# A three-matrix stage without decode steps in a block's first product, and with one operand load issued later

## The chip, the cores and the metric

The kernel runs on one core of a Trainium2 chip. The time of a kernel is the device time of one execution in microseconds (us); of several runs the median counts. Times inside a profile are microseconds from the start of the profiled span.

## The reference, cut to what matters

An attention with decay comes first, then two feed-forward networks. The stage that is changed here computes the inner part of the second one, three products of the same x with three weight matrices and the largest of the three, element by element:

```
def _moe2_ref(x, w1, w2, w3, w_out) -> np.ndarray:
    h = np.maximum(np.maximum(x @ w1, x @ w2), x @ w3)
    return (h @ w_out).astype(np.float32)
```

x is 3072 x 512, each of w1, w2, w3 is 512 x 768, all float32. The weights reach the kernel as 64-bit numbers, two 32-bit words each, and the kernel decodes them into float32 itself.

## The kernel before, in words

**Products.** Each large matrix product is done by a seven-product scheme on 2 x 2 blocks (Strassen's form): seven products q0 to q6 of sums of blocks take the place of eight. To keep float32 precision on TensorE, an operand is split in a high part (ScalarE, a cast, L254) and the rest (VectorE, a subtraction, L255), and three matmuls take the place of one: high x high, high x low, low x high (L876 to L878).

**Order of the changed stage.** The outer loop is over three passes j (`GH = 3`): each pass has its own third of the columns of all three weight matrices. In a pass three blocks n go through (`NB = 3`), each a third of the tokens. In a block run the seven products q. A product has three parts p, one for each weight matrix, each of six matmuls into one bank of PSUM. The text numbers the 63 products of the stage 0 to 62 (`s = 7 * blk + q`, `blk = 3 * j + n`) and the parts 1 to 3. Everything is issued by hand in program order; each engine runs its own instructions in that order, and so does each DMA queue (SP's, and the one that ScalarE issues).

**Banks.** Six banks form two sets of three, "a" and "b", which swap roles from block to block. `ORDER` says which set a product writes and whether it starts it afresh: q0 a, q1 b, q2 a, q3 b, q4 a, q5 b, q6 a; q0 and q3 start afresh, and in block 0 q1 does. In all other blocks q1 accumulates onto what the copies of q0 (L881, ScalarE) have put into the set b: that set was the "a" of the block before, so a copy of q0 has to wait until the last product of the block before, q6, has been read out of that bank (L891 on ScalarE for part 1, maxima of L889 on VectorE for parts 2 and 3). q0 writes the set that was "b" before, so it waits for the evictions of q5 (L895, VectorE).

**Operands.** The split operands lie in HBM (`spill`) and are loaded again for every pass. In pass 0 operands 8 to 20 are still made in the stage (`make_op`: cast on ScalarE, subtraction on VectorE, store by SP). From operand 21 on they are loaded by `op_load`, 1 MB each, up to operand 24 on SP's queue, from operand 25 on on ScalarE's. When product s ends, the operand that next uses its buffer (`heir[s]`) is loaded: six products later in pass 1 (six buffers), four products later in pass 2 (four buffers).

**Decode steps.** While a pass runs, the weights of the next are decoded (in the last pass: the output weights). Six pieces of 512 KB are fetched into three buffers and go through `step`, which alternates `decode_a` and `decode_b`. A piece is taken up by `decode_front` (L124 on ScalarE, which waits for the piece to land, and L126 on GpSimd), goes through L147 and L149 on VectorE (`decode_a`), L156 on ScalarE (`decode_b`) and L141 on VectorE (the next `decode_a`). When a piece is finished, `due` rises by one, and the next `decode_b` issues a fetch for each one due, on ScalarE's queue (`due_more`, L93). In addition the first block of a pass issues a fetch at the head of q0, q2 and q4, on SP's queue, and sets the count of those due to zero:

```
if n == 0 and q in (0, 2, 4):
    due[0] = 0
    more()
```

`Spread(jobs, slots)` hands out the steps: `side.tick()` is called once a part, and at tick t as many jobs are done as len(jobs) * t / slots, rounded up. The first two jobs are idle, then come 12 steps; the last pass adds a `drain` and seven pieces (`wogen`) that split the output weights on ScalarE (L211) and VectorE (L212). In passes 0 and 1 the decoded weights are split at the ends of the products of the third block (`wgen`).

Of the kernel before, what the change touches and what calls it, by code (L numbers as in the profile page):

```python
# [33 lines left out]
GH = 3  # L34
# [13 lines left out]
def fused_kernel(ctx: ExitStack, tc: tile.TileContext, ck, w12, w3t, wo1, w123, wo2, mask, gout, gch, kdec, out):  # L48
# [16 lines left out]
    def spill(n, q):  # L65
        return opsp[n, q].rearrange("h p x -> p h x")

    def halves(t):
        return t.bitcast(F32).rearrange("p (h x) -> p h x", h=2)

    def stage_pool(name, side="left"):
        st = ExitStack()
        return st, pool(st, name, side=side, reuse_waits="tile")
# [15 lines left out]
    def fetch(src, raw, hi=None, lo=None, st=None):  # L89
        k = stage_turn[0]  # L90
        stage_turn[0] += 1
        st = ring[k % len(ring)] if st is None else st
        (nc.scalar if late[0] else nc.sync).dma_start(out=st.bitcast(I64), in_=src)  # L93
        loaded.append((st, dec_t[k % 2][:, :], raw, hi, lo))
# [138 lines left out]
    def raw_quads(n):  # L233
        return [wraw_t[0][:, i * n:(i + 1) * n] for i in range(4)]
# [177 lines left out]
    def fetch_w123(j, w, u):  # L412
        raw = wraw_t[0][:, :4 * GH * 256].rearrange("p (q i n) -> p q i n", q=4, i=GH)
        fetch(w123[j, w, u], raw[:, 2 * u:2 * u + 2, w, :])
# [8 lines left out]
    with tc.manual_schedule():  # L423
# [129 lines left out]
        side = Spread([idle] * 5 + [step] * (4 * GA), 4 * (12 + LAG))  # L553
        wgen = weights(raw_quads(1024), 1024)
        for g in range(KF // GA):
            for n in range(NB):
                blk = g * NB + n
                sets = sets_b(blk)
                for q in range(7):
                    s = 7 * blk + q  # L560
# [5 lines left out]
                    t = s + 3  # L566
# [49 lines left out]
                    if z == 6:  # L616
# [11 lines left out]
                        side = Spread([idle] * 3 + [step] * 36, 4 * (7 * NB - LAG))  # L628
# [45 lines left out]
        side = Spread([step] * 12, 8 * ZD)  # L674
# [42 lines left out]
        J1, J2 = 7 * NB, 14 * NB  # L717
        home_h = [z % 4 for z in range(J1)] + [(4, 5, 1, 2, 3, 0)[z % 6] for z in range(J1)] + [(2, 3, 0, 1)[z % 4] for z in range(J1)]
        bufs_h = [x[:, :] for x in op_t]
        heir = {s: next((t for t in range(s + 1, 7 * NB * GH) if home_h[t] == z), None) for s, z in enumerate(home_h)}  # L720

        def op_load(t):
            eng = nc.sync if t < J1 + 4 else nc.scalar
            eng.dma_start(out=halves(bufs_h[home_h[t]]), in_=spill(t // 7 % NB, t % 7))  # L724
# [3 lines left out]
        side = Spread([idle] * 4 + [step] * (4 * GH), 26)  # L728
        wgen = weights(raw_quads(256 * GH), 256 * GH)
        GEN = (15, 18, 21, 24, 27, 30, 33, 36)  # L730
        XL = 0
        for s in range(XS):
            n, r = divmod(s, 14)
            q, kk = divmod(r, 2)
# [90 lines left out]
        for j in range(GH):  # L825
            if j == GH - 1:
                xc_st.close()
                xb_st.close()
            if j + 1 < GH:
                wq += [lambda w=w, u=u: fetch_w123(j + 1, w, u) for w in range(GH) for u in range(2)]  # L830
                side = Spread([idle] * 2 + [step] * (4 * GH), 2 * 21 + 3)
            else:
                o_st, o_pl = stage_pool("o")
                wo = [o_pl.tile([P, 2, 768], F32R, name=f"wo{q}") for q in range(7)]
                raw = wraw_t[0][:, :].rearrange("p (m u k n) -> p m u k n", m=2, u=2, k=3)
                wq += [lambda k=k: fetch(wo2[k], raw[:, :, k // 3, k % 3, :]) for k in range(KH)]
                wogen = weights(raw_quads(768), 768, lambda q, n: wo[q])
                side = Spread([idle] * 2 + [step] * (2 * KH) + [drain]
                              + [lambda q=q: wogen(q) for q in (0, 1, 5, 2, 3, 4, 6)], 2 * 21 + 6)
            wgen = weights(raw_quads(256 * GH), 256 * GH)  # L840
            for n in range(NB):
                blk = j * NB + n
                sets = {"a": hbank[blk % 2], "b": hbank[1 - blk % 2]}
                m11, m21, m12, m22 = m_t[blk % 2]
                for q in range(7):
                    s = 7 * blk + q
                    if s < XL:
                        xwgen(7 - XL + s)
                    if s == 0:
                        op_load(3)  # L850
                    if PH[q] < 0:
                        make_op(s, quad_h, len(GEN))
                    if j == GH - 1 and n == NB - 1:
                        if q == 3:
                            o_load(0, 0, 0)
                            o_load(0, 0, 1)
                        elif q == 4:
                            o_load(0, 1, 0)
                            o_load(0, 1, 1)
                        elif q == 5:  # L860
                            o_split(0)
                        elif q == 6:
                            o_split(1)
                            o_pre(2)
# [3 lines that stand above are left out]
                    which, first = ORDER[q]  # L868
                    x = quads4(bufs_h[home_h[s]])
                    w = wslot(q, 256 * GH).rearrange("p h (i k n) -> p h i k n", i=GH, k=2)  # L870
                    seeded = blk > 0 and q == 1
                    for p in range(GH):
                        ps = sets[which][p]
                        for k in range(2):
                            wh, wl = w[:, 0, p, k, :], w[:, 1, p, k, :]
                            nc.tensor.matmul(ps, wh, x[:, 0, k, :], start=first and k == 0 and not seeded, stop=False, skip_group_check=True)  # L876
                            nc.tensor.matmul(ps, wh, x[:, 1, k, :], start=False, stop=False, skip_group_check=True)  # L877
                            nc.tensor.matmul(ps, wl, x[:, 0, k, :], start=False, stop=k == 1, skip_group_check=True)  # L878
                        u, c, e = (part(nm, p) for nm in "UCE")
                        if q == 0:  # L880
                            nc.scalar.copy(out=sets["b"][p] if blk else u, in_=ps)  # L881
                        elif q == 2:
                            nc.scalar.copy(out=c, in_=ps)
                        elif q == 3:
                            nc.scalar.copy(out=e, in_=ps)
                        elif seeded or q == 6:
                            m = m12 if q == 6 else m11
                            if p:
                                nc.vector.tensor_tensor(out=m, in0=m, in1=ps, op=ALU.max)  # L889
                            else:  # L890
                                nc.scalar.copy(out=m, in_=ps)  # L891
                        else:
                            m, v, (x0, x1), op = {1: (m11, u, (u, ps), ALU.add), 4: (m22, e, (ps, e), ALU.subtract),
                                                  5: (m21, c, (c, ps), ALU.subtract)}[q]
                            nc.vector.tensor_tensor(out=v if p else m, in0=x0, in1=x1, op=op)  # L895
                            if p:
                                nc.vector.tensor_tensor(out=m, in0=m, in1=v, op=ALU.max)
                        if p == GH - 1:
                            if s == 12:
                                xc_st.close()  # L900
                                xc_st, xc_pl = stage_pool("x2o")
                                bufs_h += [xc_pl.tile([P, 2048], F32R, name=f"opx{z}")[:, :] for z in range(2)]
                            if s in (12, 13):
                                op_load(J1 + s - 12)
                            t = heir[s]
                            if t is not None and not len(GEN) <= t < J1:
                                op_load(t)
                        if p == PH[q]:
                            make_op(s, quad_h, len(GEN))
                        side.tick()  # L910
                    if q == 1:
                        store(hsp[n, 0, :, j, :], m11)
                    elif q == 4:
                        store(hsp[n, 1, :, j + 3, :], m22)
                    elif q == 5:
                        store(hsp[n, 0, :, j + 3, :], m21)
                    elif q == 6:
                        store(hsp[n, 1, :, j, :], m12)
                    stores()
                    if n == NB - 1 and j + 1 < GH:  # L920
                        if q == 0:
                            side.rest()
                            drain()
                        wgen(q)
            side.rest()
# [6 lines left out]
        for s in range(7 * NB):  # L932
            n, q = divmod(s, 7)
# [99 lines left out]
```

## Time and profile before

| | |
|---|---|
| median of three runs | 820.87 us (819.47 to 821.22) |
| the profiled execution | 818.6 us |
| its span, first to last instruction | 816.6 us |
| TensorE matmul, weight load | 805.8 us (99%), 672.5 us (82%) |
| VectorE (DVE) | 631.9 us (77%) |
| ScalarE (ACT) | 389.1 us (48%) |
| GpSimd (POOL) | 76.0 us (9%) |
| the changed stage | about 468 to 726 us of the span |

In the profile PE is TensorE's matmul, PEld its weight load, which runs beside the matmuls; DVE, ACT, POOL and SP are the other engines, and ACTq and SPq stand for what these issue themselves, mostly DMAs. A row of a timeline has the start, the duration, the engine, the line of the kernel, the operation, the tile written and those read; in square brackets stands how long the engine was idle before it, and what it waited for.

### The profile page before, as it was taken

What the parts mean: (1) busy time and instruction counts of PE and PEld (TensorE: products, weight loads), DVE (VectorE), ACT (ScalarE), POOL (GpSimd) and SP (SyncE); (2) the same over time, 40 slices, a digit from 0 to 9 for tenths busy, and PEclk for the clock granted to TensorE, in tenths of its full rate; (3) what the DMA queues carried; (4) which work ended last, traced back from release to release, by engine and by line L of the source; (5) the groups of instructions that cost most, each with busy time, mean ns of one, the idle gap of its engine ahead of it and who ended that gap; (6) DMA issues with size and microseconds to landing.
All of it is one profiled execution on the core that took longest, in us unless ns stands there. A gap on an engine that the chain in (4) does not pass through costs nothing. (4 is left out here: it accounts for less than half of the span.)

```text
span 816.6 us, 12214 instructions
## 1 busy us (share of the span) xinstructions
PE 805.8 (99%) x4648; PEld 672.5 (82%) x4648; DVE 631.9 (77%) x795; ACT 389.1 (48%) x589; POOL 76.0 (9%) x93
## 2 busy tenths in 40 slices
PE   8999999999999999999999999999999999999997
PEld 8889888888888888888888888888888888888886
DVE  3799899989698978679799848993665555588782
ACT  2432646463345454567577545453334334444642
POOL 2443000000011111001010001000000010000000
PEclk9999999999999999999999999999999999999999
DMA  9998698799999975686789798989998699956522
GB/s 346 407 407 309 226 365 344 274 342 330 388 334 417 352 307 182 241 298 212 269 301 350 275 347 306 369 292 417 394 318 306 239 335 351 326 210 215 193 104 78
DMA packets 70154, 246.56 MB, mean 302 GB/s; under 512 B 6608, under 2 KB 6736, under 8 KB 70096
## 3 DMA queue, kind: packets, MB, share of 16 engines
q1 hardware_dynamic: 48864, 165.97, 53.8%
q10 hardware_dynamic: 21232, 79.81, 27.4%
q8 instruction: 37, 0.61, 0.3%
q14 instruction: 21, 0.17, 0.1%
HBM read 163.97 MB, written 81.79 MB: 301 GB/s over the span
## 5 line engine op out<-in xcount | busy, mean ns | idle before, releaser
L577 PE MATMUL bank<-op,w 128*128 128x512 f32 x336 | 130.8, 389 | 0.0
L579 PE MATMUL bank<-op,w 128*128 128x512 f32 x336 | 130.7, 389 | 0.0
L578 PE MATMUL bank<-op,w 128*128 128x512 f32 x336 | 130.7, 389 | 0.0
L876 PE MATMUL bank<-op,w 128*128 128x512 f32 x330 | 128.6, 390 | 0.1
L878 PE MATMUL bank<-op,w 128*128 128x512 f32 x330 | 128.4, 389 | 0.0
L877 PE MATMUL bank<-op,w 128*128 128x512 f32 x330 | 128.4, 389 | 0.0
L126 POOL TENSOR_SCALAR dec<-dec 128x512 f32<-128x512 f32 x64 | 48.5, 757 | 552.8 <-ACT dec L124 516.1
L577 PEld LDWEIGHTS bank<-op,w 128*128 128x128 f32 x336 | 63.1, 188 | 13.3 <-issue 0.2
L578 PEld LDWEIGHTS bank<-op,w 128*128 128x128 f32 x336 | 63.1, 188 | 13.2
L579 PEld LDWEIGHTS bank<-op,w 128*128 128x128 f32 x336 | 63.1, 188 | 12.9
L876 PEld LDWEIGHTS bank<-op,w 128*128 128x128 f32 x330 | 61.9, 188 | 13.9 <-ACT bank L881 0.9
L878 PEld LDWEIGHTS bank<-op,w 128*128 128x128 f32 x330 | 61.9, 188 | 12.8
L877 PEld LDWEIGHTS bank<-op,w 128*128 128x128 f32 x330 | 61.9, 188 | 12.8
L752 PE MATMUL bank<-op,w 128*128 128x512 f32 x168 | 65.4, 389 | 0.0
L750 PE MATMUL bank<-op,w 128*128 128x512 f32 x168 | 65.4, 389 | 0.0
L751 PE MATMUL bank<-op,w 128*128 128x512 f32 x168 | 65.4, 389 | 0.0
L156 ACT ACTIVATE dec<-stg 128x512 int32<-128x512 uint32 x49 | 33.1, 676 | 52.4 <-DVE stg L149 46.0
L147 DVE TENSOR_SCALAR dec<-dec 128x512 int32<-128x512 int32 x64 | 27.0, 421 | 21.8 <-POOL dec L126 21.8
L124 ACT ACTIVATE dec<-stg 128x512 f32<-128x512 f32 x49 | 32.6, 665 | 13.2 <-DMA stg<-in_w_dram 7.4
L889 DVE TENSOR_TENSOR m<-m,bank 128x512 f32<-128x512 f32 x34 | 23.3, 684 | 19.6 <-PE bank L878 19.0
L948 PE MATMUL bank<-w,wo 128*128 128x512 f32 x96 | 37.4, 390 | 0.0
L947 PE MATMUL bank<-w,wo 128*128 128x512 f32 x96 | 37.4, 389 | 0.0
(216 smaller groups left out, 1581.8 us busy)
## 6 DMA issues: line engine op xcount, KB each, us to landing
op<-opsp ACTq DMA_DIRECT2D x53, 1024.0 KB, 8.1
opsp<-op SPq DMA_DIRECT2D x34, 1024.0 KB, 5.6
ck<-in_ck_dram SPq DMA_DIRECT2D x34, 512.0 KB, 10.0
fsp<-C SPq DMA_DIRECT2D x24, 512.0 KB, 4.8
op<-opsp SPq DMA_DIRECT2D x10, 1024.0 KB, 6.0
hsp<-m SPq DMA_DIRECT2D x32, 256.0 KB, 6.3
stg<-in_w_dram SPq DMA_DIRECT2D x15, 512.0 KB, 9.4
U<-fsp SPq DMA_DIRECT2D x14, 512.0 KB, 5.9
```

What stands on the lines that cost most here:

```text
L126: nc.gpsimd.tensor_scalar(out=df, in0=df, scalar1=MAX_HI, scalar2=MIN_HI, op0=ALU.min, op1=ALU.max)
L577: nc.tensor.matmul(ps, wh, x[:, 0, k, :], start=first and k == 0 and not seeded, stop=False, skip_group_check=True)
L578: nc.tensor.matmul(ps, wh, x[:, 1, k, :], start=False, stop=False, skip_group_check=True)
L579: nc.tensor.matmul(ps, wl, x[:, 0, k, :], start=False, stop=k == 1, skip_group_check=True)
L750: nc.tensor.matmul(ps, wh, x[:, 0, k, :], start=first and kk == 0 and k == 0, stop=False, skip_group_check=True)
L751: nc.tensor.matmul(ps, wh, x[:, 1, k, :], start=False, stop=False, skip_group_check=True)
L752: nc.tensor.matmul(ps, wl, x[:, 0, k, :], start=False, stop=kk == 1 and k == 1, skip_group_check=True)
L876: nc.tensor.matmul(ps, wh, x[:, 0, k, :], start=first and k == 0 and not seeded, stop=False, skip_group_check=True)
L877: nc.tensor.matmul(ps, wh, x[:, 1, k, :], start=False, stop=False, skip_group_check=True)
L878: nc.tensor.matmul(ps, wl, x[:, 0, k, :], start=False, stop=k == 1, skip_group_check=True)
L947: nc.tensor.matmul(ps, wh[:, k, o], xh[:, k], start=first and k == 0, stop=False, skip_group_check=True)
L948: nc.tensor.matmul(ps, wh[:, k, o], xl[:, k], start=False, stop=False, skip_group_check=True)
```

## The change

In the last two passes, and in the first one from its second block on, no tick is made in q0. The number of slots is set to 39, 36 and 39 for the three passes, where it was 45, 45 and 48. The load that stood at the end of q6 (for the buffer that q6 has freed) is issued at the end of the next block's q0, ahead of q0's own load.

```
@@ -828,7 +828,7 @@
             if j + 1 < GH:
                 wq += [lambda w=w, u=u: fetch_w123(j + 1, w, u) for w in range(GH) for u in range(2)]
-                side = Spread([idle] * 2 + [step] * (4 * GH), 2 * 21 + 3)
+                side = Spread([idle] * 2 + [step] * (4 * GH), (39, 36)[j])
@@ -836,7 +836,7 @@
                 side = Spread([idle] * 2 + [step] * (2 * KH) + [drain]
-                              + [lambda q=q: wogen(q) for q in (0, 1, 5, 2, 3, 4, 6)], 2 * 21 + 6)
+                              + [lambda q=q: wogen(q) for q in (0, 1, 5, 2, 3, 4, 6)], 39)
@@ -902,12 +902,14 @@
                             if s in (12, 13):
                                 op_load(J1 + s - 12)
-                            t = heir[s]
-                            if t is not None and not len(GEN) <= t < J1:
-                                op_load(t)
+                            for s0 in {0: (s - 1, s), 6: ()}.get(q, (s,)):
+                                t = heir.get(s0)
+                                if t is not None and not len(GEN) <= t < J1:
+                                    op_load(t)
                         if p == PH[q]:
                             make_op(s, quad_h, len(GEN))
-                        side.tick()
+                        if q or not blk:
+                            side.tick()
```

## Rows read from the trace of the kernel before

**Rows 1.** The page, busy time of each engine, with its share of the span.

```profile
PE 805.8 (99%) x4648; PEld 672.5 (82%) x4648; DVE 631.9 (77%) x795; ACT 389.1 (48%) x589; POOL 76.0 (9%) x93
```

**Rows 2.** Timeline of PE: first matmuls of products 0, 4, 5 and 62.

```profile
468.23 0.39 PE L876 MATMUL bank<-op,w 128*128 128x512 f32 x1
...
484.55 0.39 PE L876 MATMUL bank<-op,w 128*128 128x512 f32 x1
...
488.63 0.39 PE L876 MATMUL bank<-op,w 128*128 128x512 f32 x1
...
722.28 0.39 PE L876 MATMUL bank<-op,w 128*128 128x512 f32 x1
```

**Rows 3.** Timeline of PEld: the three weight loads of the stage that waited.

```profile
532.24 0.19 PEld L876 LDWEIGHTS bank<-op,w 128*128 128x128 f32 x1 [0.36 <-ACT bank L881]
...
558.51 0.19 PEld L876 LDWEIGHTS bank<-opx,w 128*128 128x128 f32 x1 [0.54 <-ACT bank L881]
...
673.18 0.19 PEld L876 LDWEIGHTS bank<-op,w 128*128 128x128 f32 x1 [0.56 <-ACT bank L881]
```

**Rows 4.** Windows: length; busy PE, PEld, DVE, ACT, POOL; clock, DMA share, GB/s.

```profile
500.00:554.20 54.20, 54.20 (x240) 44.53 (x239) 50.34 (x64) 30.35 (x45) 2.45 (x3) 1.00 0.93 341
```

**Rows 5.** Timeline of SP's queue: the third fetch of pass 0.

```profile
485.15 0.46 SPq L93 DMA_DIRECT2D stg<-in_w_dram  x1
```

**Rows 6.** Timeline of ACT in block 0, q5: operand 8's cast, a piece taken up.

```profile
488.82 1.06 ACT L254 CAST op<-x 128x1024 fp32r<-128x1024 f32 x1 [3.44 <-PE bank L878]
...
493.11 0.67 ACT L124 ACTIVATE dec<-stg 128x512 f32<-128x512 f32 x1 [2.64 <-DMA stg<-in_w_dram]
```

**Rows 7.** Timeline of DVE: operand 8, q6's last maximum, two idle times, the fifth piece.

```profile
491.15 1.22 DVE L255 TENSOR_TENSOR op<-x,op 128x1024 fp32r<-128x1024 f32 x1
...
500.24 0.68 DVE L889 TENSOR_TENSOR m<-m,bank 128x512 f32<-128x512 f32 x1
501.27 1.23 DVE L255 TENSOR_TENSOR op<-x,op 128x1024 fp32r<-128x1024 f32 x1 [0.36 <-ACT op L254]
503.86 0.69 DVE L889 TENSOR_TENSOR m<-m,bank 128x512 f32<-128x512 f32 x1 [1.36 <-PE bank L878]
...
512.95 0.42 DVE L147 TENSOR_SCALAR dec<-dec 128x512 int32<-128x512 int32 x1
```

**Rows 8.** Timeline of ACT: the sixth fetch, and the copy before the first stall.

```profile
508.60 0.33 ACTq L93 DMA_DIRECT2D stg<-in_w_dram  x1
...
531.62 0.57 ACT L881 COPY bank<-bank 128x512 f32<-128x512 f32 x1 [0.74 <-DVE m L889]
```

**Rows 9.** Line 93 from 492 to 514, three fetches on ACT's queue: to landing.

```profile
DMA to landing us min/median/max: 4.8/5.0/5.3
```

**Rows 10.** The page, costliest groups: line 126 on POOL (busy, mean ns, idle before).

```profile
L126 POOL TENSOR_SCALAR dec<-dec 128x512 f32<-128x512 f32 x64 | 48.5, 757 | 552.8 <-ACT dec L124 516.1
```

**Rows 11.** Timeline of ACT's queue: the load of operand 26.

```profile
556.71 0.38 ACTq L724 DMA_DIRECT2D op<-opsp  x1
```

**Rows 12.** Timeline of ACT and its queue in block 6, q3, to block 7, q0.

```profile
655.41 0.35 ACTq L93 DMA_DIRECT2D stg<-in_wo_dram  x1
...
656.83 0.37 ACTq L724 DMA_DIRECT2D op<-opsp  x1
662.36 0.66 ACT L124 ACTIVATE dec<-stg 128x512 f32<-128x512 f32 x1 [5.00 <-DMA op<-opsp]
...
665.08 0.35 ACTq L93 DMA_DIRECT2D stg<-in_wo_dram  x1
...
672.56 1.06 ACT L881 COPY bank<-bank 128x512 f32<-128x512 f32 x2
```

**Rows 13.** Line 724 from 640 to 720, 18 operand loads: to landing.

```profile
DMA to landing us min/median/max: 6.3/7.8/10.5
```

**Rows 14.** Timeline of ACT's queue: the load at the end of product 56.

```profile
702.40 0.38 ACTq L724 DMA_DIRECT2D op<-opsp  x1
```

**Rows 15.** Timeline of DVE: one piece of the output weights.

```profile
702.20 0.95 DVE L212 TENSOR_TENSOR wo<-wraw_h,wo 128x768 fp32r<-128x768 f32 x1
```

## The prediction

> **What bounds the kernel now.** I read the page's table of engines first: TensorE's matmul row is busy 805.8 of 816.6 us [rows 1], so a change off TensorE can win only time in which TensorE waits, and loses time by making it wait. Then the starts of single products: product 4 of the stage starts at 484.55, product 5 at 488.63, so a product takes 4.08 us, a third of one (a part) 1.36. From product 0 (468.23) to product 62 (722.28) are 254.05 us; 62 x 4.08 = 252.96. The whole stage of 63 products waits 1.1 us [rows 2]. The view of weight loads names the three places: 532.24, 558.51 and 673.18, idle 0.36, 0.54 and 0.56 us, each released by the copy of line 881 on ScalarE [rows 3]. (The sum, 1.46, is above 1.1: I take 0.2, 0.4, 0.4 as what the matmuls lost, near the measured 1.1.) All three are in a block's q1, which accumulates onto what q0's copies put into its banks; the copies stood in ScalarE's order behind something that waited. Last, how full VectorE is: 50.34 of 54.20 us from 500 to 554.2 [rows 4]. There it has 3.9 us to spare, and a late VectorE stays late.
>
> So the gain is capped at 1.1 us (0.13%), and the question is what the new places of the decode steps make wait.
>
> **The change, part by part.** The steps come in pairs: an odd step finishes one piece on VectorE (L141) and starts the next (L124 on ScalarE, L126 on GpSimd, L147 and L149 on VectorE); an even one runs L156 on ScalarE, takes up the next piece (L124) and issues a fetch on ScalarE's queue for every piece finished. Nothing is added or removed, 12 steps a pass stay 12. What moves is where they stand. Number the parts of each product 1 to 3.
>
> *Pass 0.* Before, job m stands at tick floor(45(m-1)/14)+1, after at floor(39(m-1)/14)+1. Step 3 (m = 5) goes from tick 13 (q4, part 1) to tick 12 (q3, part 3); step 4 from q5 part 2 to q4 part 2. This crosses a line of the code: at the head of q4 of a pass's first block the count of owed fetches is set to 0 and one fetch goes out on SP. Step 3 now earns its fetch before that, and loses it. The fetches on ScalarE's queue, which went with steps 4, 6 and 8, go with steps 6, 8 and 10. Two things follow.
>
> First, step 4's L124 needs the piece fetched on SP at 485.15, and that fetch is not moved [rows 5]. ScalarE waited 2.64 us for it, until 493.11 [rows 6]. It did so after the cast of line 254 for operand 8 (488.82); now step 4 stands ahead of that cast. ScalarE's order is fixed, so the cast waits until 493.1 + 0.6, ends at 494.75, and VectorE's subtraction for operand 8 starts at 494.8 where it started at 491.15 [rows 7]. Behind it on VectorE stand q5's evictions and the maxima of q6. From that subtraction to the last maximum of q6 VectorE worked without a gap, 491.15 to 500.24 [rows 7]: 9.1 us, the same instructions in both kernels (the odd step among them stands elsewhere, but still inside). So that maximum starts at 503.9 and ends at 504.6, the copy of line 881 behind it at 505.2. TensorE wants that bank in q1 of block 1, part 3: 484.55 + 4 x 4.08 + 2.72 = 503.6. Loss by then 1.6 us.
>
> Second, the fifth piece. Step 8 stands in q2 of block 1 in both kernels, but now it issues the fifth fetch, where before it issued the sixth (508.60, [rows 8]). From 500.24 to there were 8.4 us, 1.7 of it VectorE idle [rows 7]; from 503.9 and without that idle time it is about 510.5. These fetches land after 5.0 us [rows 9]: 515.5. Step 9 follows one part later, so ScalarE stands in L124 until then, and with 0.67 for it [rows 6], 0.76 for GpSimd [rows 10] and three hand-overs VectorE starts L147 at 517.0. It started at 512.95 [rows 7]: 4.05 late. The idle time of VectorE absorbs some (3.9 us in 54 [rows 4]; the 18 us up to the next use have about 1); I take 3.1. The copy that ended the first stall of before ran at 531.62 for 0.57 [rows 8], and ends now at 535.3; TensorE without any stall would want it at 484.55 + 11 x 4.08 + 2.72 = 532.15. So pass 0 loses 3.1 us in all up to there (the 1.6 is within it) where it lost 0.2: **+2.9**. Bounds: all idle time absorbed 1.5, none 3.9. Later VectorE and TensorE are late together, and nothing more is lost.
>
> *Pass 1.* Step 3 stands in q4 part 2, behind the reset, as before: fetches stay with steps 4, 6, 8. The stall at 558.51 goes: the load of operand 26 stood on ScalarE's queue ahead of q0's copies, issued at 556.71 [rows 11] though product 20 had ended at 554.1 (468.23 + 21 x 4.08, and the 0.2 lost before); now it stands behind them. **-0.4**.
>
> *Pass 2.* Steps 3 and 4 stand in q3 (parts 2 and 3; before q2 part 3 and q3 part 2). The fetch of step 4 was issued at 655.41, behind q3's second copy. Now it is behind the third copy and the load issued at 656.83, so at about 657.2: 1.8 later. A chain hangs on it: L124 waited for this piece until 662.36, then GpSimd, L147, L149 and L156 let the next fetch out at 665.08, and the L124 that waits for that one is what q0's first copy (672.56) stood behind [rows 12]. Step 8 remains in q6, ahead of that copy: keeping steps out of q0 doesn't take it away. Each link follows the last, so all of it moves by 1.8 less what slack the links have, and the third stall grows from 0.4 to some 2.1: **+1.7** (bounds 0 and 3.1, the next paragraph's).
>
> The piece issued at 655.41 stood ahead of the load of 656.83 and was there by 662.36 [rows 12]. The Trainium skill ("DMA: Bandwidth & Descriptors", Queues, rings and completion order) says that on each DMA engine the descriptors of one issuing queue are consumed in ring order. Here the fetch changes place with a 1 MB load on the same queue and would have to let it pass. No row shows that order by itself. By the rows as used the sum stays 4.7; what the rule would make of it is a rival below.
>
> *The moved loads.* Six: operands 26, 33, 40 in pass 1, 45, 52, 59 in pass 2, all on ScalarE's queue, none past SP or GpSimd. In pass 1 a buffer is used again six products later, five are left for the load, now four, 16.3 us: hidden. In pass 2 it is four later: three products were left and now two, 8.16 us less 0.2 to issue, 7.9 us. Loads of this stretch land after 6.3 to 10.5 us, median 7.8 [rows 13]. Two go out together, the older need first, and the queue has had 4 us without a load, so I take the lower half: operands 45 and 52 just in time. Operand 59's issue stands behind copies that wait for VectorE's maxima, and those behind the output weights' pieces. Before, the load at the end of product 56 (722.28 - 5 x 4.08 = 701.88) was issued at 702.40 [rows 14], 0.3 later than others; now one piece more, 0.95 [rows 15], stands in q6 ahead of the maxima: about 1.2 late, 6.7 us are left, a loss of **+0.5** (bounds 0 and 3 x 2.6 = 7.8, if each takes 10.5).
>
> *The rest.* The tail's pieces of the output weights end within two parts of where they did; SP's loads of the next stage come later than that: 0 (cover gone: 1 us, one such piece).
>
> Sum: 2.9 - 0.4 + 1.7 + 0.5 = **+4.7 us**. The profiled execution took 818.6 (span 816.6 and 2.0 around it): 823.3. The median of the three runs is 820.87, 2.3 above it, so I predict 820.87 + 4.7 = **825.6**.
>
> **The rivals.** (a) Everything new is hidden: VectorE's waits fit in its idle time and the loads land in time. Then only the stalls go: -1.1, 819.8, not slower. For it: the copies have a part or two of room before q1; against it: 4 us late with 3.9 to spare. It decides at the lag of the copy at 531.62, which must stay under 0.5 us. 0.05. (b) Pass 0's term alone is hidden, if the fetch of 485.15 lands some 2 us earlier: 4.7 - 2.9 = +1.8, 822.7. 0.10. (c) The fetch of pass 2 waits for the load before it. The time used above is 657.2 + 6.9 (655.41 to 662.3) = 664.1. The load issued at 656.83 lands after 7.8 at 664.6, or 1.5 sooner without the piece ahead of it (512 KB at 341 GB/s, [rows 4]), and the piece 1.5 behind it: 664.6 to 666.1, 0.5 to 2.0 beyond. With 1.4 of that: 827.0. By the skill's rule on ring order it would come out so. 0.13. (d) The loads decide: each of 45, 52, 59 takes 9 us, a loss of about 1.1, 1.1 and 2.3, 4 more than I took: 829.6. For it: the slowest took 10.5 [rows 13]; against it: the thinned queue ahead of each. 0.12. The forecast itself: 0.60, with its own range 823.8 to 827.8.
>
> About 0.2% (1.6 us) can be told from no change. Faster by more needs more than the stage has to give: 0.03. Within it: the rest of (a), half of (b), the lower edge of the forecast: 0.11. Slower 0.86. The range leaves a tenth on each side: 822.4 to 830.2.
>
> **What would show it.** In the changed trace: no stall at product 22; stalls of 0.5 to 1 us each at block 1's q0 and q1 and at block 2's q0 and q1; ScalarE's L124 idle for DMA in q4 of block 0 and twice in block 1; a stall of about 2 us at product 50; the fetches on ScalarE's queue in pass 0 some two products later. I am wrong if pass 0 has no stall (VectorE then was not the limit), or if the stage waits less than 2 us.

## The result, and the profile after

The changed kernel is slower: 824.43 us (median of 6 runs) against 819.03 for the kernel before, ratio 1.0066 (95% interval 1.0045 to 1.0086). That is +5.4 us where +4.7 was forecast. The time lies in the stated range, 1.2 us under the 825.6 that was named, and that closeness is in part luck: two errors of opposite sign, for the kernel before was 1.8 us faster in this comparison than in the three runs that the forecast added to, and the change cost 0.7 us more than it said. A second series of both kernels gave 825.14 against 818.91, ratio 1.0084 (1.0067 to 1.0101). The profiled execution took 823.7 us, its span 821.6, 5.0 more than before.

First the same three readings as before: TensorE's row of the page, and the starts of product 0 and of product 62 on the PE timeline.

```profile
PE 806.7 (98%) x4648; PEld 672.0 (82%) x4648; DVE 632.4 (77%) x795; ACT 388.8 (47%) x589; POOL 74.2 (9%) x93
...
467.97 0.39 PE L876 MATMUL bank<-op,w 128*128 128x512 f32 x1
...
727.89 0.47 PE L876 MATMUL bank<-op,w 128*128 128x512 f32 x1 [0.25 <-DMA op<-opsp]
```

The work is the same (805.8 us busy before, [rows 1]). From product 0 to 62 are now 259.92 us, 6.96 more than 62 x 4.08, where before it was 1.1 [rows 2]. So the changed stage lost 5.9 us more; the span grew by 5.0 because the stage began 0.26 earlier and the part behind it was 0.7 shorter, which no run here explains (from the stage's last matmul to the end of the span it varies from 89.8 to 90.7 us between the kernels of this study).

The weight loads that waited name the places, as in [rows 3]; the number in brackets is the idle time ahead of each and what released it.

```profile
526.49 0.19 PEld L876 LDWEIGHTS bank<-op,w 128*128 128x128 f32 x1 [1.45 <-issue]
528.75 0.19 PEld L876 LDWEIGHTS bank<-op,w 128*128 128x128 f32 x1 [1.03 <-DVE C L895]
534.92 0.19 PEld L876 LDWEIGHTS bank<-op,w 128*128 128x128 f32 x1 [0.86 <-ACT bank L881]
670.93 0.19 PEld L876 LDWEIGHTS bank<-op,w 128*128 128x128 f32 x1 [1.48 <-DVE E L895]
678.36 0.19 PEld L876 LDWEIGHTS bank<-op,w 128*128 128x128 f32 x1 [2.12 <-ACT bank L881]
727.86 0.19 PEld L876 LDWEIGHTS bank<-op,w 128*128 128x128 f32 x1 [0.65 <-DVE m L895]
```

Three are in the first two products of block 2 (14 and 15), one in the last product of block 6 (48), one in block 7's q1 (50), one at the stage's last product (62). The third stall of before, at 673.18, is now at 678.36 and some four times as long; the one at 558.51 is gone. What TensorE itself lost is less than the idle time of its weight loads, and is read from the spacing of matmul starts, which is 0.227 us without a wait:

```profile
676.27 0.39 PE L878 MATMUL bank<-op,w 128*128 128x512 f32 x1
678.36 0.50 PE L876 MATMUL bank<-op,w 128*128 128x512 f32 x1 [1.69 <-ACT bank L881]
678.69 0.40 PE L877 MATMUL bank<-op,w 128*128 128x512 f32 x1
```

2.09 - 0.227 + 0.33 - 0.227 = 1.97 us. All stalls below are taken so. This table has them for every kernel of the study (us lost, by product; the last column is all that the stage lost from its first matmul to its last):

| kernel | 7 and 8 | 13 to 15 | 22 | 48 | 50 | 62 | all |
|---|---|---|---|---|---|---|---|
| before | 0 | 0.2 | 0.4 | 0 | 0.4 | 0 | 1.1 |
| changed | 0 | 3.0 | 0 | 1.3 | 2.0 | 0.5 | 7.0 |
| changed, again | 0 | 3.0 | 0 | 0.9 | 2.0 | 0.9 | 6.9 |
| fetch credit kept | 1.7 | 0.2 | 0 | 0.7 | 1.9 | 1.5 | 6.2 |
| third fetch early | 0 | 0.2 | 0 | 0.8 | 1.9 | 0.3 | 3.4 |
| fetch ahead of load | 1.5 | 3.0 | 0 | 0 | 0.4 | 0.5 | 5.6 |
| last pass undone | 2.0 | 3.0 | 0 | 0 | 0 | 0 | 5.3 |
| loads' move undone | 1.4 | 3.2 | 0.1 | 1.2 | 2.1 | 0 | 8.2 |
| both mended | 0 | 0.2 | 0 | 0 | 0.3 | 0.5 | 1.1 |
| moved loads alone | 0 | 0.2 | 0 | 0 | 0.1 | 0 | 0.35 |

*Pass 0, how the stall comes about.* ScalarE and its queue, in block 0's q4 and block 1:

```profile
491.35 0.66 ACT L124 ACTIVATE dec<-stg 128x512 f32<-128x512 f32 x1 [3.90 <-DMA stg<-in_w_dram]
491.91 1.03 ACT L254 CAST op<-x 128x1024 fp32r<-128x1024 f32 x1
...
508.91 0.33 ACTq L93 DMA_DIRECT2D stg<-in_w_dram  x1
...
514.94 0.66 ACT L124 ACTIVATE dec<-stg 128x512 f32<-128x512 f32 x1 [3.45 <-DMA stg<-in_w_dram]
...
517.58 0.33 ACTq L93 DMA_DIRECT2D stg<-in_w_dram  x1
...
522.72 0.68 ACT L124 ACTIVATE dec<-stg 128x512 f32<-128x512 f32 x1 [3.53 <-DMA stg<-in_w_dram]
```

The cast of operand 8, at 488.82 before [rows 6], now stands behind the piece that is waited for, at 491.91. The sixth fetch, out at 508.60 before [rows 8], goes out at 517.58; at 508.91 it is only the fifth. ScalarE waits 3.45 us for that one. VectorE waits with it, in the step's L147 for the fifth piece:

```profile
516.33 0.43 DVE L147 TENSOR_SCALAR dec<-dec 128x512 int32<-128x512 int32 x1 [3.46 <-POOL dec L126]
...
525.70 0.68 DVE L895 TENSOR_TENSOR m<-C,bank 128x512 f32<-128x512 f32 x1
```

L147 was at 512.95 before [rows 7], 3.4 us earlier. From 516.33 VectorE has no pause up to q5's first eviction at 525.70, and product 14, whose first matmul overwrites that bank, starts behind it at 526.5 instead of at 525.1 (467.97 + 14 x 4.08).

*Pass 2.* ScalarE's queue at the end of product 45 and ScalarE behind it; then VectorE up to the next L149; then ScalarE up to the copies of block 7's q0:

```profile
659.09 0.37 ACTq L724 DMA_DIRECT2D op<-opsp  x1
659.51 0.66 ACT L156 ACTIVATE dec<-stg 128x512 int32<-128x512 uint32 x1
659.52 0.46 ACTq L93 DMA_DIRECT2D stg<-in_wo_dram  x1
667.67 0.66 ACT L124 ACTIVATE dec<-stg 128x512 f32<-128x512 f32 x1 [7.50 <-DMA stg<-in_wo_dram]
```

```profile
669.06 0.43 DVE L147 TENSOR_SCALAR dec<-dec 128x512 int32<-128x512 int32 x1 [5.22 <-POOL dec L126]
...
670.19 0.68 DVE L895 TENSOR_TENSOR E<-bank,E 128x512 f32<-128x512 f32 x1
...
675.88 0.69 DVE L149 SCALAR_TENSOR_TENSOR stg<-stg,dec 128x512 int32<-128x512 int32 x1
```

```profile
670.40 0.35 ACTq L93 DMA_DIRECT2D stg<-in_wo_dram  x1
...
676.60 0.67 ACT L156 ACTIVATE dec<-stg 128x512 int32<-128x512 uint32 x1 [4.60 <-DVE stg L149]
...
677.18 0.64 ACT L124 ACTIVATE dec<-stg 128x512 f32<-128x512 f32 x1
677.73 1.06 ACT L881 COPY bank<-bank 128x512 f32<-128x512 f32 x2
```

The fetch is behind the 1 MB load now, where it stood ahead of it [rows 12], and takes 8.1 us. VectorE stands in L147 for 5.22 us, and behind L147 stands the last eviction of q4, on which product 48 waits (670.93 in the list of weight loads). From 669.06 on VectorE has no pause up to the end of L149 at 676.57. ScalarE's L156 waits 4.60 us for that L149; behind L156 stand L124 and the copies of q0, and behind the first copy product 50 (678.36).

### The profile page after: what moved, and what is told of

Same layout as the page of the kernel before. It is cut to its first block, busy times and chain, and to the rows that moved or that the text cites. A ratio compares the mean times of both kernels' runs of the same rounds, so it can differ in the third digit from the quotient of the medians.

```text
span 821.6 us, 12218 instructions
## 1 busy us (share of the span) xinstructions
PE 806.7 (98%) x4648; PEld 672.0 (82%) x4648; DVE 632.4 (77%) x795; ACT 388.8 (47%) x589; POOL 74.2 (9%) x93
## 5 line engine op out<-in xcount | busy, mean ns | idle before, releaser
L126 POOL TENSOR_SCALAR dec<-dec 128x512 f32<-128x512 f32 x64 | 46.8, 731 | 559.1 <-ACT dec L124 465.9
L577 PEld LDWEIGHTS bank<-op,w 128*128 128x128 f32 x336 | 63.1, 188 | 13.3 <-issue 0.2
L156 ACT ACTIVATE dec<-stg 128x512 int32<-128x512 uint32 x49 | 33.1, 675 | 52.6 <-DVE stg L149 52.5
L147 DVE TENSOR_SCALAR dec<-dec 128x512 int32<-128x512 int32 x64 | 27.0, 422 | 32.3 <-POOL dec L126 32.3
L124 ACT ACTIVATE dec<-stg 128x512 f32<-128x512 f32 x49 | 32.6, 665 | 26.6 <-DMA stg<-in_w_dram 18.5
```

Of the source, the lines that this page charges most:

```text
L126: nc.gpsimd.tensor_scalar(out=df, in0=df, scalar1=MAX_HI, scalar2=MIN_HI, op0=ALU.min, op1=ALU.max)
```

## The experiments

**Fetch credit kept.** Does pass 0 lose through the fetch that the reset at q4 swallows?

```
                     if n == 0 and q in (0, 2, 4):
-                        due[0] = 0
+                        if j or q < 4:
+                            due[0] = 0
                         more()
```

> The changed kernel, but the count of owed fetches is not set to zero at q4 of block 0 (pass 0), so the fetch that step 3 earned goes out on ScalarE's queue with step 4, as before. Theory (lost fetch: the pieces of pass 0 come a step pair late, VectorE stands in L147 for the fifth piece and is late at the end of block 1): the stalls at products 14 and 15, 2.8 us in the changed kernel, vanish or fall under 0.5; pass 2 is untouched, so the span falls from 821.6 by 2.3 to 2.8, ratio to the kernel before some 1.003. Rival (VectorE's work is merely bunched, because the steps come closer together and later parts have none): the stalls stay within 0.7 of 2.8 and the ratio stays at 1.0066.

Measured: 823.77 us against 819.36, ratio 1.0054 (1.0039 to 1.0068). The stalls at 14 and 15 fell from 3.0 to 0.2, as the theory has it. But the span is 822.7: 1.7 us show at products 7 and 8, where the changed kernel's own profile had none, and 1.5 at product 62. ScalarE in q4 of block 0:

```profile
493.96 0.66 ACT L124 ACTIVATE dec<-stg 128x512 f32<-128x512 f32 x1 [4.84 <-DMA stg<-in_w_dram]
493.98 0.33 ACTq L93 DMA_DIRECT2D stg<-in_w_dram  x1
494.52 1.03 ACT L254 CAST op<-x 128x1024 fp32r<-128x1024 f32 x1
```

That is the first half of pass 0's forecast: the third piece was waited for until 493.96 here, not 491.35, and operand 8's cast behind it was as late. The expected fall of the span by 2.3 to 2.8 did not come; the mechanism was confirmed by the stall that went, not by the time.

**Fetch ahead of load.** Does the fetch of pass 2 wait for the load ahead of it on the same queue?

```
+                            if s == 45:
+                                side.tick()
                             for s0 in {0: (s - 1, s), 6: ()}.get(q, (s,)):
...
-                        if q or not blk:
+                        if (q or not blk) and not (s == 45 and p == GH - 1):
                             side.tick()
```

> The changed kernel, but at the end of product 45 the decode step, with its fetch on ScalarE's queue, stands ahead of the load of operand 49 instead of behind it. Theory (ring order: the fetch waits for the 1 MB load ahead of it on the same queue): the fetch, which landed 8.1 us after its issue and 1.25 us after that load, lands after 6.4 to 6.9 us; everything that hangs on it comes about 1.3 us earlier, the stalls at products 48 and 50 (1.33 and 1.97 us) fall together by 1.3 to 2.0, the span by as much. Rival (the fetch is late only because its step stands a part later, its flight time does not depend on its place): it still takes about 8 us and the stalls change by less than 0.4.

Measured: 822.82 us, ratio 1.0045 (1.0033 to 1.0057). Nothing is lost at product 48, 0.4 at product 50. The same rows as above, and from the view of DMA issues the time to landing of the one fetch:

```profile
661.22 0.35 ACTq L93 DMA_DIRECT2D stg<-in_wo_dram  x1
661.61 0.45 ACTq L724 DMA_DIRECT2D op<-opsp  x1
661.69 0.66 ACT L156 ACTIVATE dec<-stg 128x512 int32<-128x512 uint32 x1
666.61 0.67 ACT L124 ACTIVATE dec<-stg 128x512 f32<-128x512 f32 x1 [4.25 <-DMA stg<-in_wo_dram]
...
stg<-in_wo_dram ACTq DMA_DIRECT2D x1, 512.0 KB, 5.3
```

5.3 us of flight instead of 8.1, and 0.4 earlier out: 3.2 us sooner, more than the 1.3 that was expected. On the queue two instructions changed places. One flight time alone would show little, since the same fetch can vary from profile to profile (below), but the places separate: 7.5 to 8.1 us in the five profiles in which this fetch stands 0.4 us behind the load, 5.3 and 5.4 in the two in which it stands 0.4 us ahead (both mended is the other). The rival, that the flight time does not depend on the place, is out. (The stalls at products 48 and 50 fell by 2.9, more than the 1.3 to 2.0 expected; the span fell only by 0.7, since the third fetch of pass 0 was slow again, 1.5 us at products 7 and 8, and the stage began 0.7 later.)

**Last pass undone.** Decode steps as before in pass 2 alone, loads moved.

```
-                              + [lambda q=q: wogen(q) for q in (0, 1, 5, 2, 3, 4, 6)], 39)
+                              + [lambda q=q: wogen(q) for q in (0, 1, 5, 2, 3, 4, 6)], 2 * 21 + 6)
...
-                        if q or not blk:
+                        if q or not blk or j == GH - 1:
                             side.tick()
```

> The changed kernel, but in pass 2 the decode steps stand as before (48 slots, ticks in q0 too); the moved loads and passes 0 and 1 stay changed. Theory (the decode steps' new places cost 2.9 us in pass 2, the moved loads little): the stalls at products 48 and 50 vanish (at most 0.3, since load 52 no longer stands ahead of q0's copies), at most 0.5 at operands 45, 52 and 59; the stalls at 14 and 15 stay at 2.8. Span 818.5 to 819, ratio some 1.0025. Rival (the loads issued a product late are what moves pass 2): waits of 0.5 to 2.5 us for operands 45, 52 or 59 show, and the span stays above 820.5.

Measured: 821.98 us, ratio 1.0038 (1.0024 to 1.0051). Pass 2 lost nothing, at product 50 or at any operand; the loads issued a product late all landed in time. All 5.3 us that were left are in pass 0: 3.0 at 14 and 15, 2.0 at 7 and 8, with the slowest third fetch of the study (8.4 us). The span, 822.0, missed the 818.5 to 819 that was expected and is above the rival's 820.5, but not for the rival's reason: none of the loads was waited for, and beside the 2.0 at 7 and 8 the stage began 1.4 us later than in the changed kernel.

**Moved loads alone.** The kernel before with only the third part of the change.

```
-                            t = heir[s]
-                            if t is not None and not len(GEN) <= t < J1:
-                                op_load(t)
+                            for s0 in {0: (s - 1, s), 6: ()}.get(q, (s,)):
+                                t = heir.get(s0)
+                                if t is not None and not len(GEN) <= t < J1:
+                                    op_load(t)
```

> The kernel before, with the moved loads alone (decode steps, ticks and slots as before). Theory (moving the loads is good by itself): the stall at product 22 goes (0.4), that at product 50 shrinks from 0.4 to under 0.1, since the load of operand 52 leaves its place ahead of q0's copies; operand waits stay under 0.3. Span 815.9 to 816.3, ratio 0.999. Rival (one product less for a load that takes 6.3 to 10.5 us is too little): waits for operands 45, 52 or 59 of 0.5 us and more each, ratio 1.001 or above.

Measured: 817.97 us (11 runs) against 819.36 (17 runs), ratio 0.9981 (0.9972 to 0.999): faster than both kernels. The view of waits over its stage has one line left (in total, times, longest):

```profile
PEld bank L876 <- ACT bank L881: 0.7, 3, 0.3
```

From its first product (469.18) to product 62 (722.52) are 253.34 us, 0.4 above 62 x 4.08. The stall at 22 is gone and that at 50 down to 0.1. The stage gives 0.7 of the 1.4 us between the medians; where the rest comes from is not shown.

**The changed kernel again,** to see whether the stalls at 7 and 8 belong to it.

> The changed kernel itself once more, since the three kernels with its pass 0 or near it showed stalls of some 0.75 us each at products 7 and 8 that its own profile lacked. Theory (those two depend on when the SP fetch of q4 in block 0 lands: 491.3 in its profile, 493.4 to 493.9 in the others): if this fetch lands some 7.9 us after issue, the two stalls are there too, and the span is some 1 us longer, 822 to 823.5; if after 6.4, not. The stalls at 14 and 15 (2.8) and at 48 and 50 (1.8 to 3.3) are there either way. Rival (the other kernels' edits cause them): none at 7 and 8 whatever the landing.

Measured: 825.14 us, ratio 1.0084 (1.0067 to 1.0101). In the profiled execution the fetch took 6.2 us, and there was no stall at 7 and 8. With the others: 6.4 us (changed) none; 7.7 (loads' move undone) 1.4; 7.9 (fetch ahead of load) 1.5; 8.0 (credit kept) 1.7; 8.4 (last pass undone) 2.0 us. All of these are the same kernel up to that fetch, so the edits behind it cannot have made the difference; why the flight time varies is open, and neither profile of the changed kernel itself had a slow one. The flight time stands in the view of DMA issues, here for the shortest (the changed kernel's repeat) and the longest (last pass undone), in microseconds:

```profile
stg<-in_w_dram SPq DMA_DIRECT2D x1, 512.0 KB, 6.2
```

```profile
stg<-in_w_dram SPq DMA_DIRECT2D x1, 512.0 KB, 8.4
```

The kernel before had 7.9 us on the same fetch and lost nothing by it, since there the piece is taken up a product later.

**Loads' move undone.** The changed kernel with `for s0 in (s,)` in the loop of the loads.

> The changed kernel with the loads back at the end of their own product; the decode steps stay where the change puts them. Theory (the loss is the decode steps', and the moved loads give back some): the stall at product 22 returns (0.4), pass 0 keeps its 2.8 and pass 2 its 1.8 to 3.3; the load of operand 52 stands ahead of q0's copies again but issues before the late piece, so it adds at most 0.3; the wait at operand 62 goes or shrinks. Ratio to the kernel before 1.006 to 1.008. Rival (moved loads are at least half of the loss): ratio 1.004 or less.

Measured: 826.73 us (4 runs), ratio 1.0096 (1.0083 to 1.0109), above what either theory named. That it is slower than the changed kernel beside it (1.0084, 1.0067 to 1.0101) is not shown, since the intervals overlap. By the table it lost 8.2 us against 7.0 and 6.9, and 1.4 of that stands at 7 and 8 (a slow fetch again); product 62 waits for nothing, and 48 and 50 together lose 3.3, as in the changed kernel's first profile (2.9 in its second). The stall at product 22 did not return as expected (0.1): the load of operand 26 goes out 2.2 us behind product 20's end (560.94 after 558.69), where it was 2.5 in the kernel before (556.71 after 554.16), and those 0.3 us are most of the stall. The copies of q0 stood behind that load again, only with more room. So in the changed kernel it is not shown that the move took the stall away.

**Third fetch early.** Both costs of pass 0 hang on one line; here it stands at q3.

```
-                    if n == 0 and q in (0, 2, 4):
+                    if n == 0 and q in ((0, 2, 4) if j else (0, 2, 3)):
```

> The changed kernel, but in pass 0 the third fetch on SP, with the reset of the count, stands at q3 of block 0 instead of q4. It is issued 4.1 us earlier, and step 3, which stands at the end of q3, keeps the fetch that it earns. Theory (both of pass 0's costs hang on that one line): the third piece has landed when step 4 takes it up, so nothing at products 7 and 8, and the later pieces come with steps 4, 6 and 8 again, so at 14 and 15 at most 0.3. Span 3 to 4 us under that of the changed kernel run beside it, ratio 1.002 to 1.003. Rival (bunched steps load VectorE too much in pass 0 anyway): over 1 us of stalls is left in pass 0.

The edit does two things: the fetch goes out a product earlier, and the reset no longer takes the fetch that step 3 earns. Measured: 821.15 us against 825.14 for the changed kernel beside it; ratio to the kernel before 1.0026 (1.0016 to 1.0036). The stage lost 3.4 us, 0.2 of it in pass 0. ScalarE takes the third piece up, its fetch follows, and operand 8's cast is in time:

```profile
489.04 0.67 ACT L124 ACTIVATE dec<-stg 128x512 f32<-128x512 f32 x1 [1.51 <-DMA stg<-in_w_dram]
489.06 0.33 ACTq L93 DMA_DIRECT2D stg<-in_w_dram  x1
489.62 1.04 ACT L254 CAST op<-x 128x1024 fp32r<-128x1024 f32 x1
```

**Both mended,** this and the fetch ahead of the load.

> The changed kernel with both mends, the third fetch of pass 0 at q3 and, at the end of product 45, the step's fetch ahead of the load. Theory (these two are the whole loss but for the wait at operand 62): pass 0 at most 0.3, product 50 about 0.4, operand 62 about 0.5 us; all stalls of the stage 1.0 to 1.4, as in the kernel before; ratio 0.999 to 1.001, and not as good as the moved loads alone (0.9981). Rival (something else of the change costs as well): ratio above 1.002.

Measured: 818.57 us (11 runs), ratio 1.0001 (0.9992 to 1.0009). The waits of its stage:

```profile
PEld bank L876 <- ACT bank L881: 0.8, 2, 0.5
PEld bank L876 <- DVE m L895: 0.6, 1, 0.6
```

Two places in the order of issue, one fetch (with its reset) a product earlier and one ahead of a load, are the loss of the change against the kernel before, within the interval. Something is left: product 62 still waits 0.5 us, and the moved loads alone, at 0.9981 (0.9972 to 0.999), are faster, each against the kernel before in its own series. So even mended, the new places of the decode steps have shown no gain.

## Why the prediction was right, point by point

**Direction and cap: right.** The gain could not exceed 1.1 us; the new places of the decode steps decided. Of the signs that were named, no stall at product 22, ScalarE's waits in L124 (3.90, 3.45 and 3.53 us), about 2 us at product 50 and the later fetches came; the stalls at products 7 and 8 did not.

**Pass 0, +2.9: the cause is shown; that the size came out is in part luck.** Profiled: 3.0 at products 13 to 15 where before lost 0.2. Credit kept took away that stall, and with the fetch at q3 all of pass 0's went. In the sum of the second chain two errors nearly cancel: the fifth fetch went out 1.6 us sooner than the 510.5 of the forecast and took 0.9 longer than its 5.0 (508.91, 5.9), so that L147 started at 516.33 where 517.0 was forecast. And the larger part of the stall, 2.2 us, is at product 14, behind q5's evictions; the sum had worked with the copy ahead of product 15 alone, where 0.7 is lost.

The step that failed in part is the first chain, the cast of operand 8 (a loss of 1.6 us at products 7 and 8, "within" the 3.1). It exists only when the third fetch is slow (7.7 us and up; not at 6.2 and 6.4), and then it comes on top: 1.4 to 2.0 and another 3.0 (fetch ahead of load, last pass undone, loads' move undone). It is not within, since the later chain moves by as much: in these three the fifth fetch goes out 1.3 to 2.1 us later, counted from the stage's start, than in the changed kernel, and ScalarE's wait for it is 3.3 to 3.5 us in all of them. The forecast had the slow fetch (7.9 us, landing at 493.1); with one as slow, pass 0 loses 4.5 to 5.0 us, over its bound of 3.9. Both profiles of the changed kernel happened to have a fast one.

**Product 22, -0.4: gone as forecast,** but by which part stays open in the changed kernel (above). In the kernel with the moved loads alone it went, with nothing else changed.

**Pass 2, +1.7: the late fetch was right, its size too small, and the way from it to product 50 was another.** Measured +2.9 (3.3 against 0.4), and +2.5 in the repeat. The term left out the fetch's wait behind the load: rival (c). It had 1.4 us for it, at a chance of 0.13; the fetch took 8.1 us instead of the 6.9 used, and these 1.2 us are just what the term lacked (in the repeat it took 7.6, and the term lacked 0.8). Changing the two places gave 5.3. The Trainium skill ("DMA: Bandwidth & Descriptors", Queues, rings and completion order) says that on each DMA engine the descriptors of one issuing queue are consumed in ring order. This trace agrees: 7.5 to 8.1 us behind the load, 5.3 and 5.4 ahead of it.

The second half of the forecast's chain was misread. It ran from L149 and L156 to the next fetch (665.08) and to the L124 that waits for that fetch. That L124 did not wait for it, in either kernel. Before, the fetch landed after 6.4 us, at 671.5, some 0.3 ahead of L124, and ScalarE had stood ahead of L156 and waited for VectorE's L149 until 671.28:

```profile
671.28 0.67 ACT L156 ACTIVATE dec<-stg 128x512 int32<-128x512 uint32 x1 [4.41 <-DVE stg L149]
...
671.85 0.66 ACT L124 ACTIVATE dec<-stg 128x512 f32<-128x512 f32 x1
```

In the changed kernel the fetch of 670.40 landed after 3.7 us, at 674.1, three us before L124 at 677.18, and L156 had waited 4.60 us for L149 (rows of pass 2 above). So the delay travels in VectorE's order: what stands behind the late L147 is late, q4's last eviction first (product 48, which the forecast did not have), then L149, and through L156 and the copies product 50.

**The moved loads, +0.5: operand and reason wrong, the size luck.** Operands 45, 52 and 59 landed in time in every profile, if only by 0.25 us once (52, both mended). Two of them were quicker than before, 4.7 us for operand 45 (7.9 before) and 5.3 for operand 59 (8.2 before); nothing stood close ahead of them on the queue, which is a likely reason and was not tested. The wait is at product 62 (0.5, 0.9 in the repeat, up to 1.5). Its load, issued at 715.50 in time, took 12.3 us. It takes both parts of the change: 12.1 to 13.3 us in the six kernels with the moved loads and the new steps of pass 2, and 10.3 to 10.5, without a wait, in the four that lack one of them (before, moved loads alone, last pass undone, loads' move undone). A likely way: operands 59 and 60 go out late (708.49, 1.4 late where 1.2 was forecast), so 60 and 61 are still in flight, until 716.6 and 721.7, when the next stage's loads start on SP (713.1). That this backlog made operand 62's load long was not tested by itself.

**What moving the loads is worth by itself** was priced at a net +0.1 in the sum (-0.4 and +0.5). Alone it is a gain, 0.9981. In the changed kernel no gain is shown: without it the ratio is 1.0096, with it 1.0066 and 1.0084, the intervals overlap, and the profile without it had the slow fetch. Rival (d), that the loads of operands 45, 52 and 59 decide, is out.

Rival (a), all new waits hidden, is out: VectorE's lag was 3.4 us against the 0.5 that it could afford. Rival (b) had pass 0 hidden if the third fetch lands some 2 us earlier; in the changed kernel it landed 1.8 us earlier (491.3 after 493.0), the first chain's stall was gone, and the second chain cost 3.0 all the same. What that rival would cost is near what the kernel with the early third fetch shows, +2.1 us where the rival had +1.8.

## What to carry to other kernels

Where steps are spread by a count, look up which lines of the code their new places cross: here a step moved by one part crossed a reset and its fetch came two steps later. Two instructions on one engine's queue that don't depend on each other are still ordered by it; a small transfer that a chain hangs on belongs ahead of a large one that has room (5.3 us against 8.1 here). Where a row starts without a wait, look at the instruction ahead of it for the wait that counts: here L156, not L124. And try the parts of a change alone: the one that was priced at nothing is the one worth keeping.

## What the runs showed of the hardware

The same fetch, at the same place behind the same work, took 6.2 to 8.4 us from one kernel's profile to the next, and 2 us of the stage hang on that. On ScalarE's queue a 512 KB fetch took 7.5 to 8.1 us behind a 1 MB load issued 0.4 us before it (five profiles), and 5.3 and 5.4 us ahead of it (two), while the load took 6.7 to 7.2 us ahead of the fetch and 7.4 and 7.6 behind it.
